# Writing each tile's rows of x as two DMAs of 64 rows, a tick apart

## The chip, the cores and the metric

The kernel runs on one core of a Trainium2 chip. The metric is the time of one execution on the device, in microseconds (us); less is better. Before the change it is 537.08 us, the median of three runs (534.24 to 539.2).

A core has five engines that run apart from each other and meet at semaphores: TensorE (PE in the profile, with its weight loads as PEld), VectorE (DVE), ScalarE (ACT), GpSimd (POOL) and SyncE (SP). SP does no arithmetic here. It issues nearly all transfers between HBM and the on-chip memory, one after the other in program order; the transfers themselves are then moved by 16 DMA engines.

## The reference

Block-sparse attention, and a mixture of experts behind it:

```python
scores = scale * np.matmul(q, k.transpose(0, 1, 3, 2))          # q: 4 batches, 8 heads, 768 rows, 64
mask = np.abs(blk_i - blk_j) <= 1                               # blocks of 32 rows
mask |= (blk_i == 0) | (blk_j == 0) | (blk_i == 23) | (blk_j == 23)
mask[rows of qb, rows of kb] = True                             # 3 sampled kb for each qb
attn_out = softmax(np.where(mask, scores, -1e9)) @ v
x = attn_out.transpose(0, 2, 1, 3).reshape(3072, 512)
logits = x @ w_gate + modality_bias[modality_id]                # 8 experts
e_idx = np.argmax(logits, axis=1)
out[rows of e] = gate_w * (np.maximum(x[rows of e] @ w1[e], 0) @ w2[e])
```

The rows of x that go to one expert are known only once the attention has been worked out, so x is written to HBM row by row and gathered from there by expert.

## The kernel before, in words

**Tiles.** The 3072 rows of x form 24 tiles of 128 rows, numbered tau = 0 to 23 in two halves of 12 (two batches each). A tile `xr` is 128 x 513 float32: 512 values of x and, in the last column, the gate's weight, which is worked out later. Tiles 0 and 12 (`xrd`) hold the first and the last block of each batch, which attend to everything ("dense"). The other 22 come from the "groups" g = 0 to 21, two blocks of queries each ("sparse"). `xr` has five buffers in turn (`NXR`), `xrd` one.

**The tick loop.** The attention is a software pipeline, written out by a loop over ticks `t`. In each tick a scores step (S), a masking step (M), an exponential (X), a transpose (T), a copy (A), the weighing of v (W with the shared keys, line 579, and V with the group's own keys, line 588), the division (O), the turning of x for the gate (Y) and the gate (G) are issued, each for an item that entered some ticks earlier. A sparse group is four items, so four ticks. Between these steps there are eight places, and `hook(place)` issues there what `side(tick, f, place)` has put down: loads, copies on POOL, pieces of the routing. The order on each engine is the order of these calls; nothing is reordered afterwards.

**The loads of a group** are issued by SP around its place in the loop: the queries (`q_raw`, line 143), the values of the neighbouring blocks (lines 495 and 496, 128 KB each) and the values of the six sampled blocks (line 520, 128 KB each, at an address that SP has read from memory with the load of line 512). For the second half the dense keys and values come in as well (lines 156 and 162, 256 KB each). Near the end the first expert's weights are loaded in halves (line 710). POOL copies keys between buffers (lines 465, 469, 481) and the values shared with the group before (line 503).

**The rows of x.** When a pair of tiles has been routed, `write` takes the weights and calls `put_row` for the two tiles, some ticks later. `put_row` does not write at once: it looks for the next ticks that lie `XD[0]` = 7 ticks behind the end of a group, takes the first of them for the first tile of the pair and the second for the second, and has SP issue the write there (line 1235, 256.5 KB). Where no such tick is left the write is issued at once. `written[tau]` notes the tick.

**Who waits for x.** The experts' groups of 256 rows are gathered by POOL (line 735). The first gather reads tiles 0 to 15 and the second tiles 0 to 17, while the attention still runs; the later ones read all 24. The program's order for the first one asks that the last write lie more than four ticks back:

```python
TES = (16, 18)                     # tiles that the first and the second gather read
def settled():
    return all(x in written for x in range(TES[0])) and t > max(written[x] for x in range(TES[0])) + 4
def rows(g):
    if now["gather"] == g and ready[g] and (g != 1 or tail[1]) and (g or settled()):
        gather(g)
```

On the chip a gather waits for the semaphores of the writes that it reads. A new tile's division (line 441, on DVE) waits until the write that last read its buffer has landed.

**SP's semaphores.** SP's transfers use eight semaphores in turn (DMAHW0 to DMAHW7 in the instruction order), and each transfer waits for the one eight places before it, which used the same semaphore, to have landed.

After the attention (from about 230 us) the experts run: three passes of float32r matmuls (lines 753 to 755 and 768 to 770) for each weight, with SP, ACT and DVE supplying split weights, POOL gathering x and scattering the results.

Of the kernel before, what the change touches and what calls it, by code (L numbers as in the profile page):

```python
# [20 lines left out]
P = 128  # L21
# [55 lines left out]
XD = (7, 7)  # L77
# [11 lines left out]
def attention_moe(ctx, tc, kD, qD, qH, v0, v1, blocks, modality, w_gate, bias, w1, w2, out):  # L89
    nc = tc.nc  # L90
# [4 lines left out]
    x_d = dram.tile([NTOK, HD + 1], F32, name="x_d")  # L95
# [23 lines left out]
    with ExitStack() as actx:  # L119
# [194 lines left out]
        def write(tau, xrs):  # L314
            gs = small.tile([P, 2], F32, name="gs")
            nc.vector.tensor_reduce(gs, exs.pop(tau), axis=AX.X, op=ALU.add)
            yield
            nc.vector.tensor_scalar(gs, gs, 1e-9, None, ALU.add)
            yield
            for n in range(2):  # L320
                nc.vector.reciprocal(xrs[n][:, HD:HD + 1], gs[:, n:n + 1])
            yield
            for _ in range(LATER):
                yield
            for n in range(2):
                put_row(n, tau + n, xrs[n])
# [841 lines left out]
        xrs, turns, banks, sums, ats, gated, written = {}, {}, {}, {}, {}, set(), {}  # L1168
# [28 lines left out]
        def side(t, f, place=7):  # L1197
            work_at.setdefault((t, place), []).append(f)
# [32 lines left out]
            return all(x in written for x in range(TES[0])) and t > max(written[x] for x in range(TES[0])) + 4  # L1231

        def put_row(n, tau, xr):
            def put():
                nc.sync.dma_start(x_d[tau * P:(tau + 1) * P, :], xr)
                written[tau] = t
            spots = [last(g) + XD[0] for g in range(2 * NM) if last(g) + XD[0] > t]
            if n < len(spots):
                side(spots[n], put, XD[1])
            else:  # L1240
                put()

        def q_load(m, half):
            qraw[m, half] = fetch_q(half, m)
# [12 lines left out]
        for g in range(2 * NM):  # L1257
            half, m = divmod(g, NM)
            t = at["s", half, m, 0, 0]
# [88 lines left out]
        with man:  # L1348
            constants()
            for token in START:  # L1350
# [3 lines left out]
                elif op == "h":  # L1354
                    t = int(token[1:])
# [8 lines left out]
            t = START_TICKS  # L1364
            while t < NI + LAG["s"]["G"] + 1 or fillers or slots_todo or choosers or early:
                spot = 0
                for op in ORDER:
# [3 lines left out]
                    for kind in "ds":  # L1371
                        k = t - LAG[kind][op]
# [71 lines left out]
```

## Time and profile before

| | |
|---|---|
| median of 3 runs | 537.08 us (534.24 to 539.2) |
| the profiled execution's own time | 536.03 us |
| its span, first to last instruction | 534.3 us |
| mean granted TensorE clock | 0.987 |
| busy: PE, PEld, DVE, ACT, POOL | 514.9, 436.1, 377.2, 335.2, 214.9 us |
| transfers issued from the SP queue (kind q1) | 105.02 MB |
| writes of x (line 1235) | 24, of 256.5 KB |

The profile's page cuts the span into 40 slices of 13.4 us and gives each engine's busy share in tenths; PEclk is the clock that TensorE was granted, in tenths of full speed, and DMA the mean busy share of the 16 DMA engines. A timeline row is: start in us, length in us, engine, line, operation, tiles, count, and in brackets the idle time before it and what ended that. In brackets "issue" means that the profile shows nothing that the engine waited for. SPq is SP's queue of issues: the length of such a row is what the issue took on SP, and not the transfer, whose landing is given as a time after the issue.

### The profile page before, as it was taken

Reading aid. Unit: us, or ns where it says so; the run is one execution under the profiler, and the core shown is the slowest. Engines: PE = TensorE matmul, PEld = TensorE weight load, DVE = VectorE, ACT = ScalarE, POOL = GpSimd, SP = SyncE. Lnnn points to the kernel's source line nnn. Section 1 sums busy time; section 2 is a strip of 40 time slices with the busy share of each in tenths; the row PEclk is TensorE's granted clock in tenths of the full one; section 3 lists DMA queues with packets and bytes.
Section 4 is the critical chain, followed back from the end, with each engine's and each line's share of the span. In section 5 each row is a group of like instructions: output and inputs, shape, how many; then the busy total and the mean of one; then the engine's idle time right before and its main releaser. Section 6 shows DMA issues by size and latency. Waiting matters only on the chain.

```text
span 534.3 us, 19017 instructions
## 1 busy us (share of the span) xinstructions
PE 514.9 (96%) x7298; PEld 436.1 (82%) x7298; DVE 377.2 (71%) x1139; ACT 335.2 (63%) x765; POOL 214.9 (40%) x451
## 2 busy tenths in 40 slices
PE   7999999998999999899999999999999999999995
PEld 5667776766778777788989898998989899898984
DVE  7995698683788999867997656556565655656553
ACT  4689877884988878835456554546555454655552
POOL 3577685574468884323155022030302203030213
PEclk9999999997999999899999999999999999999998
DMA  7995887898846798965888686676758677675840
GB/s 278 339 234 153 238 244 224 243 229 223 232 126 194 198 231 252 274 193 200 238 288 303 227 261 200 237 252 202 244 177 261 203 227 242 213 246 180 257 155 23
DMA packets 49443, 119.44 MB, mean 224 GB/s; under 512 B 7744, under 2 KB 8128, under 8 KB 49344
## 3 DMA queue, kind: packets, MB, share of 16 engines
q1 hardware_dynamic: 45248, 105.02, 64.5%
q0 software_dynamic: 4096, 13.12, 7.3%
q8 instruction: 59, 0.97, 0.8%
q14 instruction: 40, 0.33, 0.2%
HBM read 105.52 MB, written 12.86 MB: 222 GB/s over the span
## 4 chain that ended last, share of the span: by engine, by line
issue 40%; PE 39%; DVE 7%; DMA 6%; POOL 6%; SPq 2%; ACT 1%; POOLq 0%; DVEq 0%; ACTq 0%
PE bank L557 7%; PE bank L532 6%; PE bank L579 4%; PE bank L588 4%; POOL slot L735 3%; DMA out<-slot,si 2%; DMA slot<-kD 2%; PE bank L605 2%; POOL out L789 2%; PE bank L595 2%; DVE y L540 2%; PE bank L753 1%; PE bank L769 1%; PE bank L770 1%; PE bank L768 1%
## 5 line engine op out<-in xcount | busy, mean ns | idle before, releaser
L724 DVE TENSOR_TENSOR slot<-slot 128x1024 fp32r<-128x1024 f32 x99 | 123.1, 1248 | 89.3 <-ACT slot L721 87.5
L721 ACT CAST slot<-slot 128x1024 fp32r<-128x1024 f32 x104 | 108.1, 1048 | 102.1 <-PE bank L754 52.1
L753 PE MATMUL bank<-slot 128*128 128x256 f32 x384 | 108.4, 282 | 0.0
L755 PE MATMUL bank<-slot 128*128 128x256 f32 x384 | 107.8, 281 | 0.0
L754 PE MATMUL bank<-slot 128*128 128x256 f32 x384 | 107.7, 280 | 0.0
L789 POOL DMA_INDIRECT out<-slot,si x20 | 25.4, 1270 | 178.6 <-ACT slot L785 175.6
L548 ACT ACTIVATE a<-y,mn 128x256 f32<-128x256 f32 x176 | 88.7, 511 | 7.7 <-DVE mn L540 7.6
L768 PE MATMUL bank<-slot 128*128 128x512 f32 x192 | 76.6, 399 | 0.0
L769 PE MATMUL bank<-slot 128*128 128x512 f32 x192 | 75.9, 395 | 0.0
L770 PE MATMUL bank<-slot 128*128 128x512 f32 x192 | 75.8, 395 | 0.0
L753 PEld LDWEIGHTS bank<-slot 128*128 128x128 f32 x384 | 72.3, 188 | 0.6
L754 PEld LDWEIGHTS bank<-slot 128*128 128x128 f32 x384 | 72.1, 188 | 0.4
L755 PEld LDWEIGHTS bank<-slot 128*128 128x128 f32 x384 | 72.2, 188 | 0.0
L540 DVE CUSTOM_DVE_ANT_1 y<-bank,smask 128x256 f32<-128x256 f32 x176 | 66.3, 416 | 0.6 <-PE bank L532 0.2
L481 POOL COPY slot<-slot 128x128 f32 x264 | 63.9, 294 | 0.0
L562 ACT COPY at<-bank 128x512 f32<-128x512 f32 x88 | 50.6, 576 | 12.8 <-PE bank L557 12.7
L557 PE MATMUL bank<-ident,a 128*128 128x128 f32 x352 | 52.8, 284 | 0.6 <-ACT a L400 0.5
L503 POOL TENSOR_SCALAR slot<-slot 32x1024 f32<-32x1024 f32 x40 | 41.9, 1048 | 28.0 <-PE bank L588 10.2
L532 PE MATMUL bank<-slot,q_raw 64*32 64x256 f32 x1408 | 48.8, 382 | 1.1 <-DMA q_raw<-qH 0.7
L770 PEld LDWEIGHTS bank<-slot 128*128 128x128 f32 x192 | 36.1, 188 | 8.4
L557 PEld LDWEIGHTS bank<-ident,a 128*128 128x128 f32 x352 | 38.9, 142 | 4.7 <-ACT a L548 0.8
L769 PEld LDWEIGHTS bank<-slot 128*128 128x128 f32 x192 | 36.1, 188 | 7.8 <-DVE slot L724 0.4
(302 smaller groups left out, 855.4 us busy)
## 6 DMA issues: line engine op xcount, KB each, us to landing
slot<-w SPq DMA_DIRECT2D x100, 512.0 KB, 4.0
slot<-v SPq DMA_DIRECT2D x180, 128.0 KB, 4.0
x_d<-xr SPq DMA_DIRECT2D x22, 256.5 KB, 5.3
q_raw<-qH SPq DMA_DIRECT2D x22, 256.0 KB, 4.8
slot<-v SPq DMA_DIRECT2D x16, 256.0 KB, 4.9
slot<-kD SPq DMA_DIRECT2D x13, 256.0 KB, 4.2
slot<-v SPq DMA_DIRECT2D x4, 768.0 KB, 11.9
slot<-w SPq DMA_DIRECT2D x10, 256.0 KB, 5.1
```

Of the source, the lines that this page charges most:

```text
L532: nc.tensor.matmul(sp[u][32 * pr:32 * pr + 32, b * 256:(b + 1) * 256], lhsT=q[r, b * NPAIR + pr, n, :], rhs=kv[r, s0:s0 + 8, b, pr, :], st ...
L540: nc.vector.tensor_tensor_reduce(y[:, u, :].rearrange("p (s f) -> p s f", s=8), sp[u][:, b * 256:(b + 1) * 256].rearrange("p (s f) -> p s ...
L548: nc.scalar.activation(a[:, u, :], y[:, u, :], AF.Exp, bias=mn[:, u:u + 1], scale=-1.0, accum_out=total[:, u:u + 1])
L557: nc.tensor.transpose(tp[:, k:k + P], a[:, u, c * P:(c + 1) * P], ident)
L721: nc.scalar.copy(h, s)
L724: (eng or (nc.gpsimd if n in POOL_SPLITS else nc.vector)).tensor_tensor(l, s, h.bitcast(F32), ALU.subtract)
L753: nc.tensor.matmul(o, lhsT=h[:, fs], rhs=xh[g % 2][:, c, :], start=c == 0 and f % 2 == 0, stop=False)
L754: nc.tensor.matmul(o, lhsT=h[:, fs], rhs=xl[g % 2][:, c, :], start=False, stop=False)
L755: nc.tensor.matmul(o, lhsT=l[:, fs], rhs=xh[g % 2][:, c, :], start=False, stop=c == 3 and f % 2 == 1)
L768: nc.tensor.matmul(o, lhsT=hh[0][:, f, ts_], rhs=h[:, fs], start=f == 0, stop=False)
L769: nc.tensor.matmul(o, lhsT=hh[0][:, f, ts_], rhs=l[:, fs], start=False, stop=False)
L770: nc.tensor.matmul(o, lhsT=hl[f // 4][:, f % 4, ts_], rhs=h[:, fs], start=False, stop=f == 7)
```

## The change

A write of x that is put off to a later tick is no longer one DMA of 128 rows but two of 64 rows. The first is issued at the tick and place of the old one, the second one tick later at the same place. `written[tau]` is noted with the second. A write that is issued at once stays whole.

```diff
         def put_row(n, tau, xr):
-            def put():
-                nc.sync.dma_start(x_d[tau * P:(tau + 1) * P, :], xr)
-                written[tau] = t
+            def put(r0, r1):
+                nc.sync.dma_start(x_d[tau * P + r0:tau * P + r1, :], xr[r0:r1, :])
+                if r1 == P:
+                    written[tau] = t
             spots = [last(g) + XD[0] for g in range(2 * NM) if last(g) + XD[0] > t]
             if n < len(spots):
-                side(spots[n], put, XD[1])
+                for k in range(2):
+                    side(spots[n] + k, lambda k=k: put(P // 2 * k, P // 2 * k + P // 2), XD[1])
             else:
-                put()
+                put(0, P)
```

On PE, ACT, DVE and POOL the instructions and their order are the same as before; only the semaphores that some of them wait for are other ones. On SP there are 20 DMAs more: 20 of the 24 tiles are split, and the last four are written whole.

The first place is SP's queue around the write of tile 15, the last tile that the first gather reads. Here are the rows before the change (the text in brackets names the semaphores that a row waits for; line 710 loads expert weights, line 520 sampled values):

```order
L710 DMA slot<-w 128x512 [waits DMAHW0_49]
L1235 DMA x_d<-xr 128x513 [waits DMAHW1_49,DVE_49]
L495 DMA slot<-v 32x1024 [waits DMAHW2_49,PE_49,Pool_49]
L496 DMA slot<-v 32x1024 [waits DMAHW3_49]
L520 ISA
L520 DMA slot<-v 32x1024 [waits DMAHW4_49]
```

And the same place with the change:

```order
L710 DMA slot<-w 128x512 [waits DMAHW7_49]
L1235 DMA x_d<-xr 64x513 [waits DMAHW0_49,DVE_49]
L495 DMA slot<-v 32x1024 [waits DMAHW1_49,PE_49,Pool_49]
L496 DMA slot<-v 32x1024 [waits DMAHW2_49]
L1235 DMA x_d<-xr 64x513 [waits DMAHW3_49]
L520 ISA
L520 DMA slot<-v 32x1024 [waits DMAHW4_49]
```

The second 64 rows stand behind the loads of lines 495 and 496 and ahead of the six loads of line 520. The first half carries the wait for DVE; the second waits for its semaphore alone.

The second place is POOL's queue at the first gather, before the change (`gi_e` holds the rows to gather, line 503 copies shared values between two buffers):

```order
L735 DMA slot<-x_d,gi_e_77 128x513 [waits DMAHW1_49,DMAHW3_49,DVE_49,DMAHW7_49,Activation_49,Pool_49]
L735 DMA slot<-x_d,gi_e_77 128x513
L503 TENSOR_SCALAR slot<-slot 32x1024 [waits DMASW1_49,DMAHW3_49,DMASW0_49,PE_49]
L503 TENSOR_SCALAR slot<-slot 32x1024 [waits DMAHW2_49]
L503 TENSOR_SCALAR slot<-slot 32x1024 [waits DMAHW5_49,PE_49]
```

And with the change:

```order
L735 DMA slot<-x_d,gi_e_77 128x513 [waits DMAHW1_49,DMAHW3_49,DMAHW0_49,DMAHW5_49,DVE_49,DMAHW6_49,Activation_49,Pool_49]
L735 DMA slot<-x_d,gi_e_77 128x513
L503 TENSOR_SCALAR slot<-slot 32x1024 [waits DMASW1_49,DMAHW2_49,DMASW0_49,PE_49]
L503 TENSOR_SCALAR slot<-slot 32x1024 [waits DMAHW1_49]
L503 TENSOR_SCALAR slot<-slot 32x1024 [waits DMAHW5_49,PE_49]
```

Nothing has moved here; the gather waits for two more of SP's semaphores, those of second halves. In both versions the copy behind the gathers waits for DMASW0 and DMASW1, the semaphores of the two gathers themselves.

The third place is the end of SP's work for the attention, from the last three loads of sampled values on. Before:

```order
L520 DMA slot<-v 32x1024
L1235 DMA x_d<-xr 128x513 x2
L717 ISA
L717 DMA slot<-w 128x2x512
L717 ISA
```

With the change:

```order
L520 DMA slot<-v 32x1024
L1235 DMA x_d<-xr 64x513 x4
L717 ISA
L717 DMA slot<-w 128x2x512
L717 ISA
```

The writes of tiles 18 and 19 are four DMAs in a row, so that their second halves follow the first at once. The last loads of line 520 now have 18 more DMAs ahead of them on SP than before.

## The prediction

> **What bounds the kernel now.** I read the page first, for the engine that is busy throughout; then the timeline of TensorE for its pauses; then SP's and POOL's queues, since the change touches only what SP issues.
>
> ```profile
> span 534.3 us, 19017 instructions
> ...
> PE   7999999998999999899999999999999999999995
> ...
> PEclk9999999997999999899999999999999999999998
> ...
> q8 instruction: 59, 0.97, 0.8%
> ```
>
> TensorE is busy nearly everywhere, so whatever delays it adds to the time, and whatever delays another engine costs nothing until TensorE waits for it. The clock dips in two slices. Both dips follow a pause of TensorE in the attention:
>
> ```profile
> 121.60 1.65 PE L579 MATMUL bank<-slot,at 128*64 128x64 f32 x25 [2.65 <-issue]
> ...
> 218.07 0.43 PE L588 MATMUL bank<-slot,at 128*32 128x64 f32 x16 [1.83 <-issue]
> ...
> 219.97 1.96 PE L579 MATMUL bank<-slot,at 128*64 128x64 f32 x32
> ...
> 120.00:140.00 20.00, 18.11 (x358) 13.36 (x358) 10.43 (x44) 12.22 (x39) 10.76 (x34) 0.83 0.84 226
> ...
> 122.00:124.00 2.00, 2.00 (x27) 1.88 (x24) 0.00 (x0) 0.00 (x0) 2.00 (x10) 0.50 1.04 258
> ...
> 220.00:222.00 2.00, 2.00 (x37) 1.88 (x36) 2.00 (x8) 1.25 (x5) 1.49 (x2) 0.50 1.08 332
> 222.00:224.00 2.00, 2.00 (x13) 2.00 (x14) 0.96 (x2) 0.89 (x2) 0.00 (x0) 0.67 1.00 245
> ```
>
> The last four rows are stretches: busy time of five engines, then granted clock, DMA share and GB/s. Both pauses break a run of equal matmuls in the middle (25 of 32 and 16 of 64 are left), wait for nothing that the profile shows, and fall where the DMA engines are full (shares of 1.00 to 1.08 beside them). They look like a wait for instructions. The Trainium skill (Runtime: NRT & Kernel Launch, Instruction fetch mechanics) says that instructions are refilled by DMA in blocks of 16 KiB, at a cost that is mostly hidden. The q8 row (packets, MB, share of the DMA engines) fits the size, 0.97 MB in 59 packets; the two pauses show that here it is not always hidden. After each pause the clock was 0.50 for a while. Over 120 to 140 us, 0.83 of full clock is 20 x 0.17 = 3.4 us lost, so the first pause cost 2.65 + 3.4 = 6.1 us in all. The second cost 1.83 + 2 x 0.50 + 2 x 0.33 = 3.5 us.
>
> **What is added.** Twenty DMAs on SP, and no bytes. What one takes on SP is read from the queue:
>
> ```profile
> L1235 SPq DMA_DIRECT2D x_d<-xr x22: 330/376/1727, 77.9 to 259.0; - x22
> ...
> 201.82 0.38 SPq L1235 DMA_DIRECT2D x_d<-xr  x1
> 202.30 0.38 SPq L495 DMA_DIRECT2D slot<-v  x1
> 203.12 0.33 SPq L496 DMA_DIRECT2D slot<-v  x1
> 203.65 0.33 SPq L520 DMA_DIRECT2D slot<-v  x1
> ```
>
> From the write of tile 15 to the next issue it is 202.30 - 201.82 = 0.48 us; the row of 330/376/1727 ns (least, median, most) says that the issue itself is usually 0.38 us of it. So 20 x 0.48 = 9.6 us are added to SP's queue. SP waits for PE in between, which swallows lateness, so what counts is how much gathers between one such wait and the next. The last stretch is the one to work out, for it ends against TensorE:
>
> ```profile
> SPq L1235 <- DVE mn L540: 1.5, 1, 1.5
> SPq L710 <- DMA slot<-w: 1.4, 1, 1.4
> SPq L520 <- DMA slot<-w: 0.9, 1, 0.9
> ...
> SPq L520 <- DMA x_d<-xr: 0.4, 2, 0.2
> ...
> 186.00:226.00 40.00, 0.96 0.93 250
> ```
>
> These are SP's waits between 186 and 226 us. The one of 1.5 us for DVE stands at its start, in the write of tile 13 (and swallows what came before). Behind it SP waits almost only for transfers to land, which is the wait for one of the eight semaphores, with the DMA engines 0.93 busy. In that stretch five second halves are added (tiles 13 to 17): 5 x 0.48 = 2.4 us later at its end if nothing gives, nothing if the waits for landings shrink by as much, since the bytes are the same. I take the middle, 1.2 us.
>
> **Where it meets TensorE: the first gather.** POOL's gather reads tiles 0 to 15, and tile 15's write is the last of them to land:
>
> ```profile
> DMA to landing us min/median/max: 6.1/6.1/6.1
> ...
> L735 POOLq EVENT_SEMAPHORE  x3: 17/43/43, 208.0 to 208.1; - x3
> ...
> 209.03 1.19 POOL L735 DMA_INDIRECT slot<-x_d,gi_e  x1 [4.01 <-DVE mn L540]
> ...
> 217.02 4.54 POOL L503 TENSOR_SCALAR slot<-slot 32x1024 f32<-32x1024 f32 x4 [5.54 <-DMA slot<-x_d,gi_e]
> ...
> L496 SPq DMA_DIRECT2D slot<-v x1: 332/332/332, 203.1 to 203.1; - x1
> ...
> DMA to landing us min/median/max: 5.6/5.6/5.6
> ...
> L520 SPq DMA_DIRECT2D slot<-v x1: 325/325/325, 203.7 to 203.7; - x1
> ...
> DMA to landing us min/median/max: 5.4/5.4/5.4
> ```
>
> The first landing is that of tile 15's write: 201.82 + 6.1 = 207.9 us, and POOL's wait for its semaphores ends at 208.0. (The view puts the 4.01 us down to DVE, but that row's idle time ends only as the issue begins; the semaphore rows show the transfer.) Then come the two gathers, their landing, and four copies of line 503 that the order puts behind both landings, the first two for group 20, the others for group 21. The first two end about half of 4.54 us in, at 219.3 us. Group 20 is weighed on TensorE at 219.97 us, so the slack is 0.65 us: this is the narrowest place in the path of x.
>
> The second half of tile 15 is issued where the first load of line 520 stood, at 203.65 us if SP is on time. Its neighbours landed at 203.12 + 5.6 = 208.7 and 203.65 + 5.4 = 209.1 us, so I take 209.1: 1.2 us later than now. With tiles 13 and 14 ahead SP is up to 2 x 0.48 = 0.96 us late there, so 1.2 to 2.1 us, and I take 1.6. Less the slack, TensorE waits 0.55 to 1.5 us, say 0.95 us, in front of group 20's weighing. The pause of 1.83 us stands ahead of that place. If it went away, TensorE would reach the weighing earlier and wait there instead, so that pause is worth little to win.
>
> The Trainium skill has a rule against this very change (DMA: Bandwidth & Descriptors, Rules for kernel authors): two transfers to disjoint halves of the partitions only serialize, and one of 128 partitions is the better. Its fit for another queue (same page, Anatomy of one DMA) is 2.0 us fixed plus 0.3 us for 128 KB and 0.6 us for 256 KB, by which, as an estimate, a half issued 1.83 us later would land 1.5 us later, for 0.85 us of waiting in place of 0.95; the trace's landing of 6.1 us is far from its 2.6 us, and I go by the trace.
>
> **Where it meets TensorE: the last values.** The last load of line 520 in the attention is awaited by the last group's weighing:
>
> ```profile
> L520 SPq DMA_DIRECT2D slot<-v x1: 316/316/316, 224.8 to 224.8; - x1
> ...
> DMA to landing us min/median/max: 5.1/5.1/5.1
> ...
> 230.29 1.22 PE L588 MATMUL bank<-slot,at 128*32 128x64 f32 x63 [0.39 <-issue]
> ```
>
> It lands at 224.8 + 5.1 = 229.9 us, and TensorE, which stopped after one of 64 matmuls, goes on at 230.29. There is no slack: SP's lateness of 0 to 2.4 us (1.2 taken) comes out on TensorE, less what TensorE has by then lost at the gather, since both are one delay seen twice. So the two places together cost the larger, 1.2 us, between 0 and 2.4 us.
>
> **The first half.** Between 60 and 127 us SP is late by up to five second halves, 2.4 us, when it issues the last dense keys of the second half, at 105.7 us. POOL waits for them, and TensorE for POOL:
>
> ```profile
> L156 SPq DMA_DIRECT2D slot<-kD x2: 422/862/1301, 102.8 to 105.7; - x2
> ...
> 110.02 2.13 POOL L469 TENSOR_SCALAR slot<-slot 128x256 f32<-128x256 f32 x5 [2.25 <-DMA slot<-kD]
> 112.09 2.88 POOL L481 COPY slot<-slot 128x128 f32 x12
> 115.06 4.47 POOL L503 TENSOR_SCALAR slot<-slot 32x1024 f32<-32x1024 f32 x4
> ...
> 117.01 1.09 PE L532 MATMUL bank<-slot,q_raw 64*32 64x256 f32 x32
> ```
>
> Group 11's keys are ready at 112.09 + 2.88 = 115.0 us and its scores start at 117.01: 2.0 us of slack against 2.4 at most. The first two copies of line 503 end near 117.3 us, and group 9 is weighed from about 118.5 us (its 25 matmuls of 121.60 us stand behind the pause that began at 121.60 - 2.65 = 118.95 us): 1.2 us of slack, so up to 1.2 us are lost. But the pause of 2.65 us comes seven matmuls into that weighing, and if it ends with a transfer it does not move when TensorE arrives late. I take 0.2 us, between 0 and 1.2.
>
> What remains has one answer each. The second half of a tile frees its buffer later, by about the 1.83 us above; the profile shows no wait for these writes on DVE, and tiles come some 8 us apart with five buffers. The second gather waits for tile 17, but TensorE's progress releases it later still. Tiles 20 to 23 are whole, so the later gathers see nothing new. The load of lines 495 and 496 get 128 KB less ahead of them; no engine waits for these.
>
> **The sum**, against the profiled execution, whose own time is 536.03 us: 1.2 + 0.2 = 1.4 us more, 537.4 us. The median of the runs is 537.08, 1.05 us above that execution, so I forecast 538.5 us. The ends of the sum are 0 and 2.4 + 1.2 = 3.6 us, and 1.7 us on top if a wait at the gather keeps the clock at 0.50 again as long as the second pause did (2 x 0.50 + 2 x 0.33): 537.1 to 542.4 us.
>
> **The rivals.** *Nothing is felt* (537.1 us): the waits for landings give way as the queue gets lighter by half a tile, and tile 15's second half lands hardly later than its neighbours did. The DMA share of 0.93 speaks for it, the missing slack in front of group 20 against it. Chance 0.19; the forecast's own mechanism has 0.60.
>
> *A pause goes* (531.0 us, -1.1%): if instructions wait behind data, then a write of 256 KB that is cut in two just ahead of the first pause lets the block through in time, and 6.1 us are saved. Tile 6 is in fact written 1.1 us ahead of that pause:
>
> ```profile
> 117.82 0.35 SPq L1235 DMA_DIRECT2D x_d<-xr  x1
> ```
>
> Against it: the bytes stay, and they follow some two microseconds later. Chance 0.08.
>
> *A long wait halves the clock* (slower): all five second halves come through, TensorE waits 2.4 us for the last values and 1.2 us in the first half, and the wait at the end is followed by a halved clock, as the pause of 2.65 us was, for 3.4 us. That gives 2.4 + 1.2 + 3.4 = 7.0 us, 544.1 us, +1.3%. It decides from an idle time of about 1.8 us on, the shorter of the two that were followed by 0.50. Chance 0.13.
>
> That the change does not do what it says can be left out: SP's order shows the 20 DMAs.
>
> **Chances and range.** About 1%, 5.4 us, is what a measurement of this kernel tells from no change; the three runs before lie 5.0 us apart. Faster by more than that is the lost pause alone, 0.08; slower the halved clock, 0.13; within 1% the rest, 0.79. For the range I go from 534.5, which allows a median as low as the lower runs before, to 542.5 us, the upper bound of the sum; the pause that goes and the halved clock are left out of it.
>
> **What would show it.** In the changed kernel's profile: line 1235 with 44 issues; POOL's semaphores for the first gather passed at 209 to 210 us and not at 208.0, against the same tile's first half; an idle time of TensorE in front of the weighing of group 20 (line 579 near 220 us) of about 1 us that is released by POOL; the last load of line 520 issued 0 to 2.4 us later against the write of tile 13. The forecast is wrong if the pauses of 2.65 and 1.83 us have gone or new ones stand elsewhere, since those are larger than all of its terms, or if TensorE's idle time at group 20 and at the last group is unchanged.

## The result and the profile after

The changed kernel takes 544.55 us (median of 6 runs, 540.29 to 547.87) against 539.22 us for the kernel before, run beside it: a ratio of 1.013, with a 95% interval of 1.0087 to 1.0173. A second measurement, later and beside other kernels, gave 1.0132 (1.0069 to 1.0196). The ratios, here and below, are of the fast executions alone (those within 1.5% of the fastest of their kernel) while the medians are of all, so the quotients of the medians are lower, 1.0099 and 1.0094. So the change costs 0.9 to 1.3%, 5 to 7 us, where the forecast was 1.4 us (538.5 us, against a median before of 537.08 us) and "within 1%".

Two executions of the changed kernel were profiled, one of 547.87 us and one of 540.76 us: the longest and the shortest of the six in their measurements. The page of the first:

```profile
span 546.2 us, 19056 instructions
...
PE   7999999999699998699999999999999999999995
...
PEclk9999999999799998989999999999999999999999
...
q1 hardware_dynamic: 45568, 105.02, 65.6%
```

The bytes of the data queue (105.02 MB) are those of before; it has 320 packets more (45248 before), 16 for each added DMA. TensorE's weak slices are now the 11th, the 16th and the 17th of 40 (137 to 150 and 205 to 232 us), all in the attention. The experts behind it have not changed. The last group's weighing, which goes on at 230.29 us before, stands here in the timeline of TensorE of the first and the second profile:

```profile
242.15 1.07 PE L588 MATMUL bank<-slot,at 128*32 128x64 f32 x55 [0.15 <-issue]
...
235.07 1.15 PE L588 MATMUL bank<-slot,at 128*32 128x64 f32 x51 [1.17 <-issue]
```

From there to the end of the span it is 304.0 us before (534.3 - 230.3), 304.0 and 303.9 us after (546.2 - 242.2, 539.0 - 235.1), but for a few matmuls within that group by which the rows begin apart. All that was lost was lost in the attention.

SP's issues of line 1235 in the first profile, least, median and most in ns:

```profile
L1235 SPq DMA_DIRECT2D x_d<-xr x40: 430/452/1748, 78.0 to 270.8; - x40
...
L1235 SPq DMA_DIRECT2D x_d<-xrd x4: 451/460/517, 68.2 to 185.5; - x4
```

There are 44, as there should be. But a half takes 452 ns to issue (median) and a whole tile took 376. Half the rows are not half the work for SP; they are more than the whole.

The rows that the prediction named, POOL's gather and the copies behind it, with TensorE's weighing of group 20, first in the profile of 547.87 us and then in that of 540.76 us:

```profile
217.98 1.18 POOL L735 DMA_INDIRECT slot<-x_d,gi_e  x1 [8.60 <-DMA slot<-v]
...
227.95 4.40 POOL L503 TENSOR_SCALAR slot<-slot 32x1024 f32<-32x1024 f32 x4 [7.52 <-DMA slot<-v]
...
230.16 0.48 PE L579 MATMUL bank<-slot,at 128*64 128x64 f32 x2 [2.04 <-POOL slot L503]
```

```profile
206.98 1.17 SPq L1235 DMA_DIRECT2D x_d<-xr  x1
...
213.15 1.18 POOL L735 DMA_INDIRECT slot<-x_d,gi_e  x1 [6.01 <-DMA slot<-v]
...
221.40 4.39 POOL L503 TENSOR_SCALAR slot<-slot 32x1024 f32<-32x1024 f32 x4 [5.79 <-DMA slot<-x_d,gi_e]
...
223.61 2.02 PE L579 MATMUL bank<-slot,at 128*64 128x64 f32 x32 [2.96 <-POOL slot L503]
```

TensorE now waits 2.04 and 2.96 us in front of group 20, released by POOL's line 503, where before it waited for nothing. But before, it had paused for 1.83 us just ahead of that place, at the 49th of 64 matmuls of line 588; at the same matmul the pause is 1.15 us in the first profile and missing in the second. In the second profile tile 15's second half is issued at 206.98 us (the whole tile stood at 201.82) and the gather starts at 213.15 us (209.03 before). TensorE's waits for line 503 over the whole attention (us in all, times, longest), first and second profile, where the kernel before had one of 0.32 us:

```profile
PE bank L579 <- POOL slot L503: 4.0, 3, 2.0
...
PE bank L579 <- POOL slot L503: 4.1, 2, 3.0
```

How the losses lie in time is seen in the stretches. Each row has the busy time of TensorE, its weight loads, DVE, ACT and POOL, then the granted clock, the DMA share and GB/s; first before, then the two profiles after:

```profile
120.00:128.00 8.00, 6.40 (x53) 4.62 (x53) 1.28 (x7) 3.60 (x12) 4.49 (x17) 0.57 1.01 263
140.00:150.00 10.00, 10.00 (x277) 8.17 (x273) 6.84 (x37) 8.71 (x29) 4.26 (x16) 1.00 0.56 164
230.00:238.00 8.00, 7.71 (x128) 7.46 (x129) 5.48 (x21) 3.42 (x6) 1.98 (x2) 1.00 0.51 145
```

```profile
120.00:128.00 8.00, 7.97 (x188) 5.62 (x182) 5.84 (x24) 6.30 (x20) 7.19 (x20) 1.00 0.80 214
140.00:150.00 10.00, 7.32 (x110) 5.59 (x111) 3.36 (x18) 2.37 (x9) 5.24 (x13) 0.66 0.74 208
230.00:238.00 8.00, 7.61 (x117) 7.08 (x121) 6.35 (x29) 5.98 (x16) 2.18 (x3) 0.57 0.91 245
```

```profile
120.00:128.00 8.00, 7.72 (x184) 5.50 (x180) 4.55 (x18) 5.04 (x17) 7.21 (x20) 1.00 0.94 225
140.00:150.00 10.00, 10.00 (x256) 7.80 (x254) 5.80 (x29) 6.08 (x23) 4.95 (x16) 0.88 0.65 188
222.00:230.00 8.00, 6.37 (x124) 5.93 (x127) 6.45 (x28) 6.11 (x16) 3.55 (x4) 0.79 0.89 233
```

The pause of before at 119 us with its halved clock (0.57 over 120 to 128) is gone in both profiles. In the first one a new pause stands at 139 to 143 us, with the clock at 0.66 over ten microseconds, 3.4 us lost:

```profile
142.68 0.48 PE L432 MATMUL bank<-slot 128*64 128x64 f32 x4 [3.31 <-DMA slot<-v]
```

It waits for dense values (line 162), whose last load was issued at 134.99 us and not at 133.24. The second profile has no such wait, but a pause of 1.27 us before 138.65 us that nothing releases, and a clock of 0.88 there. The wait at group 20 is in both, and the clock after it is low in both: 8.00 x 0.43 = 3.4 us in the first, 8.00 x 0.21 = 1.7 us in the second.

How far TensorE is behind the kernel before is read from the matmuls of line 572, one run of eight for each group:

| start before, us | first profile | second profile |
|---|---|---|
| 128.27 | 4.23 ahead | 4.62 ahead |
| 149.18 | 2.77 behind | 1.24 ahead |
| 183.47 | 2.73 behind | 0.49 ahead |
| 215.02 (ahead of group 20's weighing) | 8.99 behind | 2.41 behind |
| 225.06 (behind it) | 12.15 behind | 4.06 behind |

One line was not looked for at all. DVE's waits, first profile:

```profile
DVE xr L441 <- DMA x_d<-xr: 7.3, 4, 2.9
```

DVE waits 7.3 us for buffers of x, of which there are five; the second half holds one for a tick longer. In the second profile it is 3.0 us. So there were two families of causes to tell apart: SP's queue got longer, and x is written later.

### The profile page after: what moved, and what is told of

It reads as the page before. It is cut to its first block, busy times and chain, and to the rows that moved or that the text cites. A ratio compares the mean times of both kernels' runs of the same rounds, so it can differ in the third digit from the quotient of the medians.

```text
span 546.2 us, 19056 instructions
## 1 busy us (share of the span) xinstructions
PE 519.3 (95%) x7298; PEld 438.6 (80%) x7298; DVE 377.1 (69%) x1139; ACT 336.1 (62%) x765; POOL 214.6 (39%) x451
## 3 DMA queue, kind: packets, MB, share of 16 engines
q1 hardware_dynamic: 45568, 105.02, 65.6%
## 4 chain that ended last, share of the span: by engine, by line
issue 39%; PE 29%; DMA 10%; DVE 7%; POOL 7%; SPq 5%; ACT 2%; POOLq 1%; DVEq 0%; ACTq 0%
PE bank L532 4%; PE bank L557 4%; PE bank L579 3%; DMA slot<-v 2%; DMA out<-slot,si 2%; POOL slot L735 2%; POOL out L789 2%; PE bank L588 2%; PE bank L432 2%; DMA slot<-w 2%; DMA x_d<-xr 2%; SPq L520 1%; PE bank L410 1%; PE bank L753 1%; PE bank L769 1%
## 5 line engine op out<-in xcount | busy, mean ns | idle before, releaser
L562 ACT COPY at<-bank 128x512 f32<-128x512 f32 x88 | 50.6, 576 | 10.8 <-PE bank L557 10.5
L532 PE MATMUL bank<-slot,q_raw 64*32 64x256 f32 x1408 | 50.3, 388 | 1.1 <-DMA q_raw<-qH 0.6
```

What stands on the lines that cost most here:

```text
L532: nc.tensor.matmul(sp[u][32 * pr:32 * pr + 32, b * 256:(b + 1) * 256], lhsT=q[r, b * NPAIR + pr, n, :], rhs=kv[r, s0:s0 + 8, b, pr, :], st ...
```

## The experiments

All ratios are to the kernel before, run on the same chip beside the kernel, with 95% intervals. Theory A is the number of issues on SP, B the tick, C the half transfer as such.

**Both halves in one place: no tick.**

```
-                    side(spots[n] + k, lambda k=k: put(...), XD[1])
+                    side(spots[n], lambda k=k: put(...), XD[1])
```

> Both halves of a tile are issued one behind the other, at the place where before the whole tile stood: SP has the same 20 more DMAs as the change, but nothing of a tile waits a tick. Three theories of the 5.3 us by which the change is slower (544.55 against 539.22). A, SP's queue: each added issue takes SP about half a microsecond, and the loads behind it are late (the dense keys of line 156 by 2.4 us, the dense values of line 162 by 1.75 us). A expects the loss to stay: 542 to 545 us, ratio about 1.01. B, the tick: the second half lands later, so a buffer of x is held longer (DVE waits 7.3 us for it in the profile) and the first gather is issued later (217.98 against 209.03 us). B expects the time of before, 539 us, and no wait of line 441 for the write. C, the transfer: a half over 64 partitions is no half as long as a whole one (320 more packets). C expects 542 to 545 us as A does, but without a later issue of the dense values.

541.75 us, ratio 1.0055 (1.0015 to 1.0094): by the point values less than half of the loss stays, though this interval and that of the change touch. B alone, which expects nothing, does not fit, and A or C alone only at the upper end. The halves take still longer to issue here (587 ns, the median), and TensorE waits on the path through the dense keys that the prediction described:

```profile
PE bank L579 <- POOL slot L503: 2.0, 1, 2.0
PE bank L532 <- POOL slot L481: 1.9, 1, 1.9
```

**The whole tile a tick later: no added issue.**

```
-                side(spots[n], put, XD[1])
+                side(spots[n] + 1, put, XD[1])
```

> The kernel before with each of the 20 tiles written whole, by one DMA, but a tick later, at the place where the change has the second half. No DMA is added. A (SP's queue) and C (the transfer) expect the time of before, 539 us within 2 us. B (the tick) expects the loss of the change or a little more, 543 to 546 us, with line 441 waiting for the write by about 7 us and the first gather at 215 us or later.

541.33 us, 1.0056 (1.0021 to 1.0091). The tick costs something without any added DMA. In its profile line 441 does not wait for a write, against B's expectation, the gather starts at 208.2 us, not late, and TensorE does not wait in front of group 20.

**A small DMA in place of the second half.**

```
+    x_s = dram.tile([32, P], F32, name="x_s")
...
+                side(spots[n] + 1, lambda: nc.sync.dma_start(x_s[tau:tau + 1, :], ident[0:1, :]), XD[1])
```

> The kernel before with its whole writes, and in addition, where the change has a second half, a DMA of 512 bytes from a constant into a buffer that nobody reads: the added issue alone, with one of the eight semaphores, without the tick and without half tiles. A (SP's queue) expects most of the loss, 542 to 545 us, and the dense keys and values issued late as in the change. B (the tick) and C (the transfer) expect 539 us within 2 us.

539.32 us, 1.0028 (0.9993 to 1.0062): not told from nothing, and not "most of the loss" either. In its profile TensorE waits longer in front of group 20 than with the change:

```profile
PE bank L579 <- POOL slot L503: 3.5, 1, 3.5
```

So a wait at that place is no measure of the loss. A single dose is too small, so the dose was raised.

**Halves for the tiles 0 to 11 only.**

```
+                for k in range(2 if tau < 12 else 1):
...
```

> Only tiles 0 to 11 are written in halves a tick apart, tiles 12 to 23 whole; so 12 of the 20 added DMAs are left, none of them behind the write of tile 12. The first gather, which waits for tile 15, sees whole tiles. If the loss comes from the dense keys and values of the first 150 us (A), 542 to 545 us are expected, and the halved clock near 142 us. If it comes from the first gather and the groups behind it (B), the time is that of before, 539 us, and the pauses at 210 and 230 us are gone.

540.14 us, 1.0038 (1.0000 to 1.0076), between the two expectations.

**The change again, beside the next three.**

> The changed kernel again, beside the three that follow. If the parts add up (the added issue alone 1.0028, the whole write a tick late 1.0056), 1.0084 is expected, 542.6 us against 538.1; if they strengthen each other, the 1.013 of its first measurement, 545 us.

543.99 us, 1.0132 (1.0069 to 1.0196), the second measurement of above. The plain sum of the two parts, 1.0084, lies within the interval.

**Three small DMAs per tile, a tick later.**

```
+                [side(spots[n] + 1, lambda k=k: nc.sync.dma_start(x_s[3 * tau + k:3 * tau + k + 1, :], ident[0:1, :]), XD[1]) for k in range(3)]
```

> The kernel before with three small DMAs of 512 bytes per tile where the change has a second half, 60 added issues and not 20, tiles whole and in time. One such DMA per tile gave 1.0028 (0.9993 to 1.0062), which leaves open whether an issue costs anything. A (SP's queue is the cost) expects three times that or more, 1.008 to 1.015, 542.5 to 546 us, and POOL's line 503 waiting for v for longer than the 14.3 us of one per tile. B (the tick) and C (the half tiles) expect no more than 1.003, 539.7 us.

551.99 us, 1.0221 (1.0141 to 1.0302). This is A: 60 issues of 512 bytes cost 2.2%, with all tiles whole and in time. It is more than three times what 20 cost (3 x 0.28 = 0.84%), which may be slack in the queue that swallows the first issues; but the upper end for 20, three times 0.62%, reaches into this interval.

**Quarters, all in one place.**

```
+                for k in range(4):
+                    side(spots[n], lambda k=k: put(P // 4 * k, P // 4 * k + P // 4), XD[1])
...
```

> Each of the 20 tiles written in four DMAs of 32 rows at one place, so 60 added issues as in the kernel with three small DMAs, but with the tile's own bytes in them and no tick. A expects the same time as there, within 1.5 us. C (a part of a tile takes longer than its share of the bytes) expects it slower by more than 1.5 us. B (the tick) expects the time of before, 538 to 540 us.

554.62 us, 1.0312 (1.0250 to 1.0374), 2.6 us above the small DMAs, as C has it. But the intervals overlap, and no property of the transfer is needed: a quarter takes SP longer to issue than a small DMA does. The first row is of the quarters, the second of the kernel with three small DMAs per tile that comes further below:

```profile
L1235 SPq DMA_DIRECT2D x_d<-xr x76: 302/422/1987, 80.1 to 280.7; - x76
...
L1239 SPq DMA_DIRECT2D x_s<-ident x60: 215/247/328, 67.7 to 247.2; - x60
```

422 against 247 ns, 60 times, is 10.5 us more of SP's time.

**The second half from ScalarE's queue.**

```
-                nc.sync.dma_start(x_d[tau * P + r0:tau * P + r1, :], xr[r0:r1, :])
+                (nc.scalar if r0 else nc.sync).dma_start(x_d[tau * P + r0:tau * P + r1, :], xr[r0:r1, :])
```

> The change, but the second half of each tile is issued by ScalarE's queue, at the same tick; SP has 24 writes as before, of which 20 are halves. A expects the loss to go, 538 to 540 us, as long as ScalarE has time for 20 issues. B (the tick) expects 1.0056 as with the whole tile a tick late, 541 us. C (the half tiles) expects 541 to 545 us.

559.79 us, 1.0417 (1.0349 to 1.0486), the slowest of all, and outside every expectation. SP's waits tell why:

```profile
SPq L1235 <- DMA x_d<-xr: 11.5, 4, 4.5
SPq L520 <- DMA x_d<-xr: 11.1, 4, 6.6
...
SPq L156 <- DMA x_d<-xr: 2.3, 2, 2.0
```

SP, which in the kernel before waits 0.7 us in all for these writes, now waits for them by microseconds. This is the wait for one of the eight semaphores, until the DMA eight before has landed. The trace shows that the eight are shared by both queues: ScalarE's halves take their turn among SP's loads, and when the DMA eight before stands in the queue of ScalarE, which comes to it later, SP waits for ScalarE. So this run put a new wait in the place of the load that it took off SP, and says nothing about A. (The Trainium skill, DMA: Bandwidth & Descriptors, Rules for kernel authors, says of spreading DMAs over several engines' queues that it only saves issue time on the sequencer. Here SP's issues between 60 and 232 us fell from 108.9 us with the change to 88.0 us, and its waits for landings rose from 8.5 to 35.9 us.)

**Where in SP's queue? Whole tiles behind the loads of line 520.** One tick could cost because the buffer is held (B1), or because the write moves from ahead of SP's wait at line 495 to behind it, in front of the loads of line 520 (B2).

```
+                written[tau] = t - 3 * (n < len(spots))
...
-                side(spots[n], put, XD[1])
+                side(spots[n] + 3, put, 4)
```

The first line keeps the order on the other engines as it was; the next experiment and the one with six buffers have its like.

> The kernel before with each of the 20 tiles written whole, by one DMA, but behind all six loads of line 520 of its group, three ticks later than before; the other engines' order is that of before. Two readings of why a whole write a tick late cost 1.0056 (541.3 us). B1, the buffer: x is held longer, DVE's line 441 waits for the write and the gather comes later. It expects three ticks to cost more than one, 1.006 to 1.017 (542 to 548 us), with line 441 waiting for the write for more than the 7.3 us of the change. B2, the place in SP's queue: before, the write was issued while SP had to wait for the loads of line 495 anyway (their buffer is released by TensorE), and a tick later it stands behind that wait and ahead of the loads of line 520, which are then late by one issue each time. It expects 1.000 here, 537 to 540 us, or less.

550.54 us, 1.0264 (1.0203 to 1.0325). B2 falls. B1 has the sign and the waits that it asked for, and a larger loss than its 1.006 to 1.017. DVE's and TensorE's waits:

```profile
DVE xr L441 <- DMA x_d<-xr: 25.3, 7, 5.4
```

```profile
201.20 0.66 PE L557 MATMUL bank<-ident,a 128*128 128x128 f32 x4 [2.04 <-DVE xr L441]
...
242.54 0.69 PE L595 MATMUL bank<-ident,xr 128*128 128x128 f32 x2 [4.10 <-DVE xr L441]
```

At three ticks the wait for the buffer goes through DVE to TensorE.

**The second half alone behind them.**

```
+                    written[tau] = t - 2 * (n < len(spots))
...
+                    side(spots[n] + 3 * k, lambda k=k: put(...), 4 if k else XD[1])
```

> The change, with the first half of each tile where it is and the second behind all six loads of line 520 of its group, two ticks later than in the change. B2 (the place in SP's queue) expects the time to fall to that of both halves in one place or below, 1.003 to 1.006, 540 to 542 us. B1 (the buffer of x held, the gather late) expects no gain on the change, 1.013 or more, 545 us.

552.08 us, 1.0289 (1.0232 to 1.0346): the same again. It goes against B2, which expected a gain on the change.

**Three small DMAs ahead of SP's wait.**

```
-                [side(spots[n] + 1, lambda k=k: ... for k in range(3)]
+                [side(spots[n], lambda k=k: ... for k in range(3)]
```

> Three small DMAs of 512 bytes per tile as in the kernel that gave 1.0221, but all at the tile's own write, ahead of SP's wait at line 495, and not a tick later, behind it. The buffers of x and the tiles' writes are those of before. B2 (the place in SP's queue) expects a clear part of the 2.2% to go, 1.003 to 1.012, 540 to 545 us. If the place doesn't matter and only the number of issues does, 1.022 again, 550 us.

549.31 us, 1.0216 (1.0164 to 1.0269), as behind the wait. The place doesn't matter, the number does. Its profile shows the path through the first half that the prediction described, with the last dense keys issued at 113.4 us (105.7 before):

```profile
L156 SPq DMA_DIRECT2D slot<-kD x17: 333/426/1362, 1.7 to 113.4; - x17
```

```profile
120.22 1.10 PE L532 MATMUL bank<-slot,q_raw 64*32 64x256 f32 x32 [2.29 <-POOL slot L481]
...
147.77 0.34 PE L432 MATMUL bank<-slot 128*64 128x64 f32 x4 [2.60 <-DMA slot<-v]
```

Group 11's scores wait for POOL's copies of the keys (line 481), and the dense weighing waits for its values, as in the first profile of the change. TensorE waits for the sampled values (line 520) as well, for which the kernel before shows no wait:

```profile
PE bank L588 <- DMA slot<-v: 4.4, 4, 2.0
```

An added DMA also takes a turn of the eight semaphores: SP's waits for landings between 60 and 232 us are 9.7 us before, 13.7 us with the three behind the wait and 19.2 us with the three ahead of it. Time on SP and turns of the semaphores are not told apart by these runs.

**Six buffers of x.** Four kernels have room for a sixth buffer (a table's memory is used again once it is dead):

```
-NAT, NXR = 5, 5
+NAT, NXR = 5, 6
```

> The change with six buffers of x and not five (the room comes from one table that was kept after its last use). B1 (the tick costs because a buffer of x is held longer) expects the tick's share to go: from 1.013 to about that of both halves in one place, 1.0055, 541 us, and no wait of line 441 for the write. If the lateness of x costs by another way (the gather, or the loads behind it), 1.013 stays, 545 us. What the added issues cost alone is untouched either way, so 1.000 is expected by neither.

> The control: the kernel before with six buffers of x. Its line 441 never waited for a write in the profile, so 1.000, 537 to 540 us.

> The whole write three ticks late, behind the loads of line 520 (1.0264 with five buffers, line 441 waiting 25.3 us for writes), with six buffers of x. B1 expects most of the 2.6% to go, 1.000 to 1.010, 538 to 543 us. If it is the late gather and not the buffer, 1.02 or more is left, 549 us.

> The whole write one tick late (1.0056 with five buffers) with six. B1 expects 1.000, 538 to 540 us; another way of lateness 1.0056, 541 us.

- The kernel before with six: 537.68 us, 0.9969 (0.9937 to 1.0002).
- Three ticks late with six: 542.91 us, 1.008 (1.0045 to 1.0116), where five gave 1.0264. DVE no longer waits for a write. B1 is shown for three ticks.
- One tick late with six: 542.06 us, 1.0062 (1.0026 to 1.0099), where five gave 1.0056. For one tick the buffer is not the cause, as line 441 had said already.
- The change with six: 543.52 us, 1.0094 (1.0057 to 1.0131), between the two expectations; its interval overlaps that of the change. Against its own control, the kernel before with six, it is 1.0094 / 0.9969 = 1.0125, nearly all of the 1.013: the sixth buffer takes nothing off the change that can be measured.

What one tick and three ticks leave is nearly the same, 0.6 and 0.8%. Both wait in front of group 20 (three ticks, then one):

```profile
224.76 1.55 PE L579 MATMUL bank<-slot,at 128*64 128x64 f32 x24 [4.57 <-POOL slot L503]
```

```profile
224.97 1.33 PE L579 MATMUL bank<-slot,at 128*64 128x64 f32 x20 [5.84 <-POOL slot L503]
```

That pointed to the gather, and so to tile 15.

**Is it tile 15?** Three kernels: halves for tiles 12 to 19 only; the change with tile 15 whole; and the kernel before with tile 15 alone a tick late.

```
+                for k in range(2 if tau >= 12 else 1):
...
+                for k in range(1 if tau == 15 else 2):
...
+                side(spots[n] + (tau == 15), put, XD[1])
```

> The counterpart of the run with tiles 0 to 11 in halves (1.0038): only tiles 12 to 19 are written in halves a tick apart, 8 of the 20 added DMAs. G, the gather: the loss comes mainly from tile 15, whose write releases the first gather, whose landing releases POOL's copies of line 503, which TensorE awaits at group 20. G expects 1.006 to 1.010 here, 542 to 544 us. S, spread: each of the 20 added DMAs costs alike, so 8 of 20, 1.004 to 1.006, 541 to 542 us.

> The change, with tile 15 alone written whole at its first half's place. G expects 1.004 to 1.009, 541 to 544 us, and a shorter wait of TensorE at line 579 of group 20 (2.0 and 3.0 us in the two profiles of the change). S expects 1.012, one of 20 less than 1.013: 545 us.

> The kernel before with tile 15 alone written a tick later, whole. All 20 a tick later gave 1.0056. G expects nearly all of that here, 1.004 to 1.006, 541 to 542 us, with a wait of TensorE at group 20 of 2 us or more. S expects a twentieth of it, 1.000, 539 us.

541.22 us, 1.0074 (1.0035 to 1.0112); 542.42 us, 1.0086 (1.0055 to 1.0118); 537.42 us, 1.0009 (0.9979 to 1.0040). The first lies in G's range of ratios (1.006 to 1.010), and its interval holds that of S (1.004 to 1.006) as well. The last one speaks against G: tile 15 late by a tick costs nothing that can be measured, although its profile has a wait at that very place:

```profile
223.11 1.17 PE L579 MATMUL bank<-slot,at 128*64 128x64 f32 x26 [1.81 <-POOL slot L503]
```

The second one lies in G's range, with S's 1.012 outside its interval by a hair, and its wait in front of group 20 is 1.40 us, shorter than in the change, as G has it. But its interval overlaps that of the change too, so that tile 15 matters where SP is late already is likely and not shown. Early tiles alone (0.38%) and late tiles alone (0.74%) add up to 1.1%, near the 1.3% of all: the loss is spread over the attention, with more of it late than early per tile (12 tiles against 8), though the intervals of the two overlap.

## Why the prediction was wrong

**What it had right.** TensorE bounds the kernel, and the experts don't change. The path was there: SP late, tile 15's write late, gather, line 503, group 20, with its wait released by POOL. The path through the last dense keys exists too, and near its forecast: they were issued at 108.05 and 108.70 us in the two profiles (105.69 before; up to 2.4 us later was expected), and TensorE waited 0.15 and 1.14 us for line 503 in front of group 9 (0.2 taken, up to 1.2). The halved clock after a wait is there as well. The rival that counted it (544.1 us) lies 0.45 us from the result, but by luck: it put the long wait at the last values, where the profiles show idle times of 0.15 and 1.17 us that nothing releases, and not at the dense values and the gather.

**The step that failed is the size of what SP's delay and the tick cost TensorE**, the "1.2 + 0.2 = 1.4 us more" of the sum: "5 x 0.48 = 2.4 us later at its end if nothing gives", of which half was taken, with a wait of 0.95 us in front of group 20 as the narrowest place. Each part alone measured more than the sum of both: the added halves without a tick 0.55%, and the tick without an added DMA 0.56%, 3 us each, though their intervals reach down to 0.8 and 1.1 us. In the profiles TensorE lost 9.42 and 4.55 us between the rows of 183.47 and 225.06 us of the table above, where the sum had 1.2 us, and at most 2.4 + 1.7.

- The price of an issue was taken from a whole tile. Issues of halves take 452 ns and not 376, and both halves do. With the gap behind it (in the second profile the first half of tile 15 starts at 204.70 us and the next load at 205.25) a tile takes 2 x 0.55 us and not 0.48: 0.62 us more and not 0.48, so 12.4 us in all. Over 60 to 232 us all of SP's issues took 92.9 us before and 108.9 and 109.5 us after, 16 us more and not 9.6.
- The second half of tile 15 was expected at 203.65 us, 0.96 later at most. It came at 206.98 us in one profile and 212.72 us in the other. Only part of that is SP's own: the first half came at 204.70 and 211.13 us, not at 201.82, as TensorE itself was some 2 and 8 us late by then from earlier waits. The prediction took SP's wait at tile 13 to swallow all that came before. In the second profile it does (tile 13 is written at 184.1 us, 184.3 before), but what TensorE loses after that comes on top; in the first, tile 13 comes at 191.03 us.
- The landing was about right: POOL's wait for the semaphores ends at 212.2 us in the second profile and at 217.1 in the first, 5.2 and 4.4 us after the second half's issue (5.4 taken).
- So the wait at group 20 was 2.04 and 2.96 us, not 0.95, beyond the 1.8 us from which the prediction itself let the clock be halved, and the clock behind it lost 3.4 and 1.7 us. But the pause of 1.83 us ahead of that place, with its own halved clock, had cost the kernel before 3.5 us by the prediction's count. As the prediction said of that pause, where it goes, TensorE waits at the weighing instead. Net of it, by the table, the place took 3.16 us in the first profiled execution and 1.65 us in the second. Nor does the wait go with the loss between kernels: it is 3.5 us with one small DMA per tile (1.0028), 1.81 us with tile 15 alone late (1.0009), and nothing with all tiles late (1.0056).

So the sum counted two places in the second half of the attention, and the loss lies in more of them, at other places in each of the two executions.

**"The profile shows no wait for these writes on DVE"**: after the change there is one, 7.3 and 3.0 us. It was rightly left at nothing for the time of one tick (six buffers don't help the whole tile a tick late, nor the change), and would be wrong by 1.8 points for three.

**The first half**, 0.2 us: the first profile lost 3.31 us at the dense values, a place that was not on the list. SP was 1.75 us late there, and TensorE, whose pause at 119 us was missing, came more than 4 us early.

**"A pause goes"**: the pause of 2.65 us went in both profiles, and by 127 us TensorE was over 4 us ahead of the kernel before. It did not help. In the first profile all of it was gone again by 143 us. The same pause is missing also with whole tiles a tick late, and shorter (1.01 us) with one small DMA per tile, so it is not a fixed part of the kernel before but one of its profiled execution. Pauses that nothing releases did not become fewer: from 40 to 250 us they sum to 5.6 us before and to 5.3 and 6.5 us after, at other matmuls each time. The reading as a wait for instructions fits, without being shown: in the trace of the kernel before, packets of 16 KiB of q8 ended at 120.24 and 216.79 us, and the two pauses 1.36 and 1.28 us later.

That execution (536.03 us) had no wait at group 20 either, and the slack of 0.65 us was read off it. The kernel before with six buffers, 0.9969 in time, has a wait in that weighing, though for ScalarE and not for the gather:

```profile
223.74 0.48 PE L579 MATMUL bank<-slot,at 128*64 128x64 f32 x4 [1.80 <-ACT at L562]
```

The Trainium skill (DMA: Bandwidth & Descriptors, Rules for kernel authors) advises against two transfers to disjoint halves of the partitions. The sign agrees (1.013, and 1.0055 with no tick between the halves). Its reason, that both halves run on the same DMA engines and serialize, is not tried by any run here; what these runs show of a cost is on the issuing queue and in the tick.

**What stays open.** The added issues (A) are a cause: 60 small ones cost 2.2% wherever they stand, by time on SP or by turns of the semaphores. How much of the 1.3% is theirs at 20 can't be told from 0 to 0.6%, or to 0.9% for halves. The tick costs 0.56% by itself on all 20 tiles, nothing on tile 15 alone, and not by the buffer; which tiles carry it, and by which wait, was not found. Why SP needs longer to issue 64 rows than 128 was not tried.

## What to carry to other kernels

Price a split transfer by issues on the queue, at the duration of the new shape and with its own spread, and ask what share of the queue's time is left: 20 small issues cost 0.28% here, 60 cost 2.2%. Where a path has 0.65 us of slack in one profiled execution, take the slack as a random quantity, and ask what follows a wait that is longer than the one worked out: here the halved clock added 1.7 to 3.4 us. And set a new wait against what the kernel before lost at the same place, and against kernels that have the wait and not the loss. A second queue is no relief while both draw on one ring of semaphores.

## What was not expected of the hardware

- The issue of 64 rows (452 ns, and 587 with both halves in one place) is longer than that of 128 (376), that of 32 rows lies between (422), and that of one row of 512 bytes is the shortest (247, and 304 with one per tile).
- DMAs on ScalarE's queue held up SP by 11.5 us at line 1235 and 11.1 us at line 520, by the semaphores that the two queues share.
- The pause with its halved clock at 119 us came and went between kernels that do nothing different there; without it the two profiled executions of the change ran 4.23 and 4.62 us ahead, and later waits took that back.
- A pause of 1.27 us in the second profile was followed by a clock of 0.50 (139.2 to 142.2 us), where the prediction let waits of about 1.8 us and more do that.
